# One decode block on one core: ten unread products more, other left-out rows in a gather, and wq loaded in two pieces

## The chip, the core and the metric

The kernel runs on one core of a Trainium2 chip. The metric is the device time of one execution in microseconds (us). Before the change it is 1305.99 us, the median of 3 runs (1305.94 to 1306.01).

## What is computed

One decode step of a transformer block in fp32 with a batch of 2, one new token each, model width 512, 32 heads of 128 and a cache of 8192 positions. The core of the reference:

```python
def _A_ref(x, k_cache, v_cache, wq, wo):
    q = (x @ wq).reshape(B, Sq, H, Dh).transpose(0, 2, 1, 3)
    scores = jnp.einsum("bhqd,bhkd->bhqk", q, k_cache) * (Dh ** -0.5)
    p = _softmax(scores, axis=-1)
    o = jnp.einsum("bhqk,bhkd->bhqd", p, v_cache)
    return o.transpose(0, 2, 1, 3).reshape(B, Sq, H * Dh) @ wo

def _B_ref(x, w1, b1, w2, b2):
    y = _layernorm(x, axis=-1)
    h = _gelu(jnp.einsum("bsd,df->bsf", y, w1) + b1)
    return jnp.einsum("bsf,fd->bsd", h, w2) + b2

h = x + _A_ref(_layernorm(x), k_cache, v_cache, wq, wo)
out = h + _B_ref(_layernorm(h), w1, b1, w2, b2)
```

k_cache and v_cache hold 2 x 32 x 8192 x 128 numbers each, 268 MB; wq (512 x 4096) and wo (4096 x 512) hold 8.39 MB each, w1 and w2 3.67 MB each. Each is read once, some 560 MB in all.

## The kernel before

**Units.** The heads are worked through in 32 units. A unit of the first 30 is a pair of heads for one batch entry (`units`, a pair g and a batch entry b), and the last two units are one head each for both entries. A unit's keys are one load of 8.39 MB, 128 partitions of 64 KB, and its values are another.

**Loads and slots.** All large loads go into a ring of three buffers of 64 KB per partition (`slot()`, name kv): wq first (lines 213 and 214), then each unit's k and v in turn, wo, and at the end the MLP's weights. `load` (L335) issues from SP, the last units' k and v from L347. A load into a buffer waits until the buffer's former content has been used. SP issues in program order; x alone is issued by ACT (L212), and the gather of wo by GpSimd. k of unit 0 comes in two halves, and the last loads (v of the last unit, L590, and w1 and w2, L601 to L606) in several pieces.

**The start.** x is normalized by VectorE and ScalarE and transposed by TensorE (L281). GpSimd makes the identity matrix, clears a few buffers and builds three placing matrices `pm` (L240 and L242: one copy for each run of kept rows) and `ioff` (L247). TensorE makes the gather's indices from them (L286), then all of q with 32 products (L308, 64 instructions) that each contract over the 128 partitions of wq; ScalarE copies it (L311), and `make_q` (L315) spreads one unit's q over the partitions (L325).

**One unit.** VectorE multiplies the keys by q in four chunks (`multiply`, L377), GpSimd adds the halves of three of the four (`halve`, L381), VectorE sums the rest (`add_up`, L384). After the second unit of a pair come the maximum over both (L394 to L404), the exponentials on ScalarE (`exps`, L421), and the products with the values on TensorE (`values`, L454). Unit i's last act is `spare(i)`, for i from 1 to 29: unread products of 2 x 2 into a corner of a buffer that is overwritten later (L332). `SPARE` of them are spread over the 29 units.

**wo and its gather.** The rows of wo for the last 8 of 28 heads are fetched by three indirect DMAs (`load_wo`, L358) in pieces of 4 rows, 8 KB per partition. `LEFT` lists, for each of the three, the partitions that are left out. Their index lies beyond the bounds check, so nothing is moved for them. `kept` turns each list into runs, and 256 of the 384 partitions are kept. The matrices `pm` put the attention output's rows on the partitions that are loaded. The three lists hold 128 partitions in all.

**The end.** The output of attention is projected (`project_all`, L524; the last two heads by L531 and the products at L675 and L678), the MLP follows (L689 to L710), and the result is written by SP (L714).

**Waits.** The class `Waits` (L40) sees each instruction as it is made and gives it the semaphores that it must wait for. DMAs from SP and ACT take eight semaphores (`by_hard_0` to `by_hard_7`) in turn, so a DMA also waits for the one issued eight before it, unless that is known to be done.

Of the kernel before, what the change touches and what calls it, by code (L numbers as in the profile page):

```python
# [12 lines left out]
P = 128  # L13
# [4 lines left out]
NG = 4  # L18
LH = 2
WARM = 3  # L20
SPARE = 412
GP = 5
SR = 4
LW = 4
LEFT = (((7, 10), (12, 16), (20, 28), (55, 56), (68, 92), (103, 104), (108, 109), (120, 121)),
        ((7, 9), (12, 17), (20, 28), (55, 56), (68, 92), (104, 105), (112, 113), (120, 121)),
        ((6, 9), (12, 16), (20, 28), (56, 57), (68, 92), (104, 105), (119, 120)))


def kept(left):  # L30
    at, runs, n = 0, [], 0
    for a, b in (*left, (P, P)):
        if a > at:
            runs.append((at, n, a - at))
            n += a - at
        at = b
    return runs, n
# [144 lines left out]
def tile_decode_block(nc, x, k, v, wq, wo, w1, b1, w2, b2, out):  # L182
# [3 lines left out]
    DC = D // P  # L186
# [21 lines left out]
    def slot():  # L208
        return kv.tile([P, ROW], F32, name="kv", tag="kv")
# [1 line left out]
    x2 = const.tile([B, D], F32, name="x2")  # L211
    nc.scalar.dma_start(x2, x.rearrange("b s d -> (b s) d"))  # L212
    wqt = slot()
    nc.sync.dma_start(wqt, wq.rearrange("(p r) n -> p (r n)", r=DC))
    wqs = wqt.rearrange("p (r n) -> p r n", r=DC)

    wol = wts.tile([P, LW, D], F32, name="wol")
# [8 lines left out]
    oall = const.tile([P, 2, 2 * GP, B], F32, name="oall")  # L226
    NQ = len(LEFT)
    og = const.tile([P, NQ * SR + LW - LH, B], F32, name="og")
    slots = [kept(x) for x in LEFT]
    first_slot = [2 * 2 * GP * P // SR + sum(n for _, n in slots[:q]) for q in range(len(LEFT))]  # L230
    HG = H - LW
# [4 lines left out]
    pms = {}  # L236
    for x in LEFT:
        if x not in pms:
            pms[x] = const.tile([P, P], F32, name=f"pm{len(pms)}")
            nc.gpsimd.memset(pms[x], 0.0)  # L240
            for p0, s0, n in kept(x)[0]:
                nc.gpsimd.tensor_copy(pms[x][:, p0:p0 + n], ident[:, s0:s0 + n])  # L242
    pm = [pms[x] for x in LEFT]
    FAR = 4096.0
    ioff = const.tile([P, len(LEFT)], F32, name="ioff")
    for q in range(len(LEFT)):
# [83 lines left out]
    def spare(i):  # L330
        for _ in range(SPARE * i // (NU - 3) - SPARE * (i - 1) // (NU - 3)):
            nc.tensor.matmul(rowacc[:, :B], wz, wz, start=True, stop=True)  # L332
# [408 lines left out]
```

## Time and profile before

| | |
|---|---|
| median of 3 runs | 1305.99 us |
| the profiled execution | 1305.84 us |
| its span, first to last instruction | 1304.4 us |
| TensorE clock granted, mean | 0.639 |
| busy: DVE / POOL / PE / ACT | 945.3 / 444.8 / 393.2 / 52.3 us |
| bytes read from HBM | 562.06 MB |

The profile covers one execution. Its times are microseconds from the span's start unless marked ns. PE is TensorE (PEld its weight loads), DVE VectorE, ACT ScalarE, POOL GpSimd, and SP the engine that issues most DMAs. A `q` behind a name (SPq) marks its queue of instructions that aren't counted as busy. L214 is line 214 of the kernel before. The bar of the span has 40 equal slices of 32.6 us. "DMA" in it is the mean busy share of the core's 16 DMA engines in tenths, and GB/s is what they moved. In a table by stage the share and the GB/s count a packet where it starts, so a short stage can show more than 1. The chain of waits is followed back from the last instruction to what released each step. "x64" is a count, and `sm<-ident,wol` reads: written tile, then the tiles read.

### The profile page before, as it was taken

What the parts mean: (1) busy time and instruction counts of PE and PEld (TensorE: products, weight loads), DVE (VectorE), ACT (ScalarE), POOL (GpSimd) and SP (SyncE); (2) the same over time, 40 slices, a digit from 0 to 9 for tenths busy, and PEclk for the clock granted to TensorE, in tenths of its full rate; (3) what the DMA queues carried; (4) which work ended last, traced back from release to release, by engine and by line L of the source; (5) the groups of instructions that cost most, each with busy time, mean ns of one, the idle gap of its engine ahead of it and who ended that gap; (6) DMA issues with size and microseconds to landing.
All of it is one profiled execution on the core that took longest, in us unless ns stands there. A gap on an engine that the chain in (4) does not pass through costs nothing.

```text
span 1304.4 us, 7121 instructions
## 1 busy us (share of the span) xinstructions
PE 393.2 (30%) x3134; PEld 127.1 (10%) x3135; DVE 945.3 (72%) x398; ACT 52.3 (4%) x173; POOL 444.8 (34%) x145
## 2 busy tenths in 40 slices
PE   3005033330412324033330503333041331403467
PEld 1001001010100101011110100101010110101113
DVE  1988777779777778777778877777976777877831
ACT  0010000000000000000000000000000000000011
POOL 2444432244432234432234442224442224444400
PEclk9557566665666657566665656657566665756687
DMA  9999999999999999999999999999999999999998
GB/s 402 434 450 419 444 424 441 429 437 432 436 431 433 436 431 435 432 428 437 431 436 430 435 434 434 435 429 441 420 447 418 449 420 441 425 430 432 421 435 366
DMA packets 12690, 561.46 MB, mean 430 GB/s; under 512 B 1504, under 2 KB 1520, under 8 KB 2676
## 3 DMA queue, kind: packets, MB, share of 16 engines
q1 hardware_dynamic: 12224, 558.92, 99.3%
q0 software_dynamic: 432, 2.10, 0.4%
q8 instruction: 24, 0.39, 0.1%
q14 instruction: 6, 0.05, 0.0%
q10 hardware_dynamic: 4, 0.00, 0.0%
HBM read 562.06 MB, written 0.00 MB: 431 GB/s over the span
## 4 chain that ended last, share of the span: by engine, by line
DMA 47%; DVE 38%; PE 13%; ACT 1%; POOL 1%; issue 0%; SPq 0%
DMA kv<-in_A_k_cache_dram 39%; DVE kv L377 22%; DVE s L384 14%; PE so L454 10%; DMA kv<-in_A_v_cache_dram 5%; DMA kv<-in_A_wq_dram 2%; DMA kv<-in_B_w_dram 1%; ACT pt L421 1%; PE so L308 1%; POOL kv L381 1%; PE sm L404 1%; DVE gm L401 0%; PE sm L396 0%; DVE orow L474 0%; DVE mx L394 0%
## 5 line engine op out<-in xcount | busy, mean ns | idle before, releaser
L377 DVE TENSOR_TENSOR kv<-kv,qps 128x4096 f32<-128x4096 f32 x128 | 564.0, 4408 | 286.3 <-DMA kv<-in_A_k_cache_dram 261.0
L381 POOL TENSOR_TENSOR kv<-kv 128x2048 f32<-128x2048 f32 x96 | 433.5, 4523 | 788.0 <-DVE kv L377 480.7
L454 PE MATMUL so<-kv,pt 128*16 128x512 f32 (+1 forms) x2048 | 289.1, 727 | 273.5 <-DMA kv<-in_A_v_cache_dram 251.4
L384 DVE TENSOR_REDUCE s<-kv 128x32 f32<-128x2048 f32 (+1 forms) x128 | 357.2, 2811 | 0.8 <-POOL kv L381 0.6
L396 PE MATMUL sm<-ident,mx 128*1 128x128 f32 x34 | 10.5, 318 | 539.3 <-DVE mx L394 539.3
L454 PEld LDWEIGHTS so<-kv,pt 128*16 128x16 f32 (+1 forms) x2048 | 63.7, 111 | 472.4 <-DMA kv<-in_A_v_cache_dram 255.0
L396 PEld LDWEIGHTS sm<-ident,mx 128*1 128x1 f32 x34 | 2.5, 79 | 546.8 <-DVE mx L394 542.7
L459 ACT ACTIVATE ss<-so 128x512 f32<-128x512 f32 x18 | 10.7, 597 | 575.2 <-PE so L454 540.7
L408 ACT ACTIVATE nb<-sm 128x4 f32<-128x4 f32 x15 | 2.6, 173 | 624.9 <-PE sm L404 624.9
L421 ACT ACTIVATE pt<-s,nb 64x128 f32<-64x128 f32 x60 | 23.9, 399 | 1.6
L401 DVE TENSOR_REDUCE gm<-sm 1x4 f32<-1x256 f32 (+1 forms) x17 | 7.0, 412 | 18.1 <-PE sm L396 18.1
L467 PE MATMUL sm<-ss,sel 128*4 128x128 f32 x120 | 15.6, 273 | 12.1 <-ACT ss L459 12.1
L332 PE MATMUL rowacc<-wz 128*2 128x2 bf16 x412 | 14.3, 163 | 0.0
L308 PE MATMUL so<-kv,yT 128*4 128x512 f32 x64 | 9.7, 776 | 14.1 <-DMA kv<-in_A_wq_dram 14.1
L325 PE MATMUL qps<-q,pick 4*128 4x128 f32 x60 | 12.1, 327 | 0.9 <-ACT q L311 0.9
L467 PEld LDWEIGHTS sm<-ss,sel 128*4 128x4 f32 x120 | 9.3, 87 | 27.8 <-ACT ss L459 25.9
L404 PE MATMUL sm<-gm,srow 1*128 1x4 f32 (+1 forms) x34 | 9.5, 348 | 8.1 <-DVE gm L401 8.1
L332 PEld LDWEIGHTS rowacc<-wz 128*2 128x2 bf16 x412 | 11.6, 81 | 1.7
L524 PE MATMUL so<-kv,oall 128*2 128x512 f32 x40 | 6.8, 844 | 15.0 <-DMA kv<-in_A_wo_dram 15.0
L421 ACT ACTIVATION_READ_ACCUMULATOR pt<-s,nb 64x1 f32 x60 | 11.1, 185 | 0.0
L486 PE MATMUL sm<-ident,orow 4*128 4x4 f32 x20 | 2.7, 257 | 25.2 <-DVE orow L474 25.2
L404 PEld LDWEIGHTS sm<-gm,srow 1*128 1x128 f32 x34 | 8.0, 292 | 13.6 <-DVE gm L401 13.6
(122 smaller groups left out, 123.8 us busy)
## 6 DMA issues: line engine op xcount, KB each, us to landing
kv<-in_A_k_cache_dram SPq DMA_DIRECT2D x6, 4096.0 KB, 34.4
kv<-in_A_v_cache_dram SPq DMA_DIRECT2D x3, 4096.0 KB
kv<-in_B_w_dram SPq DMA_DIRECT2D x3, 1792.0 KB, 13.9
kv<-in_A_wo_dram SPq DMA_DIRECT2D x1, 5120.0 KB
kv<-in_A_v_cache_dram SPq DMA_DIRECT2D x1, 2048.0 KB, 34.9
kv<-in_A_v_cache_dram SPq DMA_DIRECT2D x1, 1536.0 KB, 34.3
wol<-in_A_wo_dram SPq DMA_DIRECT2D x2, 512.0 KB, 41.0
kv<-in_B_w_dram SPq DMA_DIRECT2D x1, 768.0 KB, 14.8
```

Source lines behind the costliest of these rows:

```text
L308: nc.tensor.matmul(so2[0][32 * n:32 * n + 2 * B].rearrange("m (j d) -> m j d", d=DH), yT[:, r, (1 - e) * B:(3 - e) * B], wqe[:, r, n, e], ...
L325: nc.tensor.matmul(QP[g][:, b], w, q2[rows, j * DH:(j + 1) * DH], start=True, stop=True)
L332: nc.tensor.matmul(rowacc[:, :B], wz, wz, start=True, stop=True)
L377: nc.vector.tensor_tensor(kc, kc, QP[g][:, b, None, :].to_broadcast([P, CH, DH]), op=ALU.mult)
L381: nc.gpsimd.tensor_tensor(kc[:, :, 0:HP], kc[:, :, 0:HP], kc[:, :, HP:DH], op=ALU.add)
L384: nc.vector.tensor_reduce(S[i][:, c * CH:(c + 1) * CH], chunk(t, c)[:, :, 0:n], axis=AX.X, op=ALU.add)
L396: nc.tensor.transpose(MT[g][:, e, :], MX[g][:, e:e + 1], ident)
L404: nc.tensor.matmul(GM[g], srow, gm, start=True, stop=True)
L421: nc.scalar.activation(ptz[b][q, :, 4 * m:4 * m + 4], s[q], AF.Exp, bias=nb[q, b, e:e + 1], scale=SCALE, accum_out=lt4[q, m:m + 1])
L454: nc.tensor.matmul(so[32 * n:32 * n + w], p[:, u, cols], t[:, (at + u) * 512:(at + u + 1) * 512], start=(b == 0 and u < NG), stop=(b == B ...
L459: nc.scalar.activation(SS[g], so2[g % 2], AF.Copy)
L467: nc.tensor.matmul(OP[g], sel4[:, :, j], sj, start=(j == 0), stop=(j == 3))
```

## The change

Three constants or lines change. The number of unread products goes from 412 to 422. The lists of left-out partitions are others, with 43, 43 and 42 entries as before; the three lists now make 10, 9 and 10 runs of kept rows instead of 9, 9 and 8. wq is loaded by two DMAs in place of one: partitions 0 to 15, then 16 to 127. All lines from 215 on move down by one.

```diff
-SPARE = 412
+SPARE = 422
...
-LEFT = (((7, 10), (12, 16), (20, 28), (55, 56), (68, 92), (103, 104), (108, 109), (120, 121)),
-        ((7, 9), (12, 17), (20, 28), (55, 56), (68, 92), (104, 105), (112, 113), (120, 121)),
-        ((6, 9), (12, 16), (20, 28), (56, 57), (68, 92), (104, 105), (119, 120)))
+LEFT = (((7, 9), (12, 15), (16, 17), (20, 28), (56, 57), (68, 92), (103, 104), (108, 109), (119, 121)),
+        ((7, 9), (12, 15), (20, 28), (55, 57), (68, 92), (104, 105), (112, 113), (119, 121)),
+        ((8, 9), (12, 16), (20, 28), (55, 56), (68, 92), (103, 104), (108, 109), (112, 113), (120, 121)))
...
     wqt = slot()
-    nc.sync.dma_start(wqt, wq.rearrange("(p r) n -> p (r n)", r=DC))
+    for p0, p1 in ((0, 16), (16, P)):
+        nc.sync.dma_start(wqt[p0:p1], wq.rearrange("(p r) n -> p (r n)", r=DC)[p0:p1])
```

## Prediction

> **What bounds the kernel now.** I read first the page's bar of the span and its DMA queues, then the chain of waits, then busy time and DMA share by stage. Of the page:
>
> ```profile
> span 1304.4 us, 7121 instructions
> ...
> DMA  9999999999999999999999999999999999999998
> GB/s 402 434 450 419 444 424 441 429 437 432 436 431 433 436 431 435 432 428 437 431 436 430 435 434 434 435 429 441 420 447 418 449 420 441 425 430 432 421 435 366
> ...
> q1 hardware_dynamic: 12224, 558.92, 99.3%
> q0 software_dynamic: 432, 2.10, 0.4%
> q8 instruction: 24, 0.39, 0.1%
> ...
> HBM read 562.06 MB, written 0.00 MB: 431 GB/s over the span
> ```
>
> The 16 DMA engines have work all the time (99.3% plus 0.4% of 16 engines' span). By stage (columns: the stretch, its length, the five engines' busy time, the granted clock, the DMA share, GB/s):
>
> ```profile
> 10.00:22.00 12.00, 0.00 (x0) 0.00 (x0) 0.00 (x0) 0.00 (x0) 0.00 (x0) 1.00 0.93 401
> 22.00:33.00 11.00, 9.74 (x64) 1.77 (x64) 0.00 (x0) 0.43 (x1) 0.00 (x0) 1.00 1.00 432
> 33.00:1200.00 1167.00, 319.70 (x2558) 101.66 (x2558) 889.16 (x335) 41.87 (x151) 415.46 (x92) 0.62 1.00 433
> 1200.00:1285.00 85.00, 47.56 (x316) 14.14 (x316) 49.33 (x35) 5.17 (x15) 22.75 (x11) 0.71 0.99 421
> 1285.00:1301.00 16.00, 13.13 (x176) 7.26 (x171) 2.29 (x9) 3.31 (x5) 0.00 (x0) 0.79 0.98 407
> ```
>
> For 1167 us the share is 1.00 at 433 GB/s, while DVE, the busiest engine, works 889.16 of them (76%). So no engine bounds the kernel; the transfers do, and each waits only for the one ahead of it on its DMA engine. The two ends of the chain of waits (start, length, what):
>
> ```profile
> 0.74 21.90 DMA kv<-in_A_wq_dram
> 22.68 9.87 PE so L308 x64
> ...
> 105.18 34.83 DMA kv<-in_A_k_cache_dram
> ...
> 1285.76 15.99 DMA kv<-in_B_w_dram
> 1301.75 0.04 issue
> 1301.79 0.55 PE qps L710 x8
> ```
>
> The span begins with wq and ends 2.65 us after the last piece of w2 has landed (1304.4 less 1301.75). A k load issued at 105.18 lands 34.83 us later. Its own bytes, 8.39 MB at 433 GB/s, take 19.4 us; the other 15.4 us are transfers queued ahead of it. So a computation that is some us late costs nothing, but a microsecond in which all DMA engines move too little is never won back: it is added to the end.
>
> **The change part by part.** The sum is made against the profiled execution, 1305.84 us (span 1304.4 and 1.44 outside it); the median of the runs shown, 1305.99, is 0.15 above it.
>
> *wq in two pieces.* The reader's side first:
>
> ```profile
> L214 SPq DMA_DIRECT2D kv<-in_A_wq_dram x1: 398/398/398, 0.7 to 0.7; - x1
> ```
>
> ```profile
> 6.84 0.80 POOL L247 TENSOR_SCALAR ioff<-pidx 128x1 f32<-128x1 f32 x3
> ...
> 7.13 1.44 PE L286 MATMUL sm<-ioff,pm 128*128 128x1 f32 x6 [2.12 <-POOL ioff L247]
> ...
> 22.68 9.74 PE L308 MATMUL so<-kv,yT 128*4 128x512 f32 x64 [14.11 <-DMA kv<-in_A_wq_dram]
> ```
>
> No product begins sooner: each L308 product contracts over all 128 partitions, so the first waits for both pieces. Behind it on PE stands everything else; ACT's copy (L311) and DVE's first multiply wait for it. SP issues one DMA more (0.398 us by the row above), so k's first halves are issued 0.4 us later; wq keeps the DMA engines busy 20 us longer than that, so it costs nothing. The eight completion semaphores are taken in turn, and every later DMA moves on by one; the DMA whose completion each one waits for (eight back) stays the same.
>
> What matters is how fast 16 partitions are filled. 1.05 MB (16 x 64 KB) at 433 GB/s is 2.42 us, the other 112 are 17.0 us, together the 19.4 us of the whole. The trace has no such transfer: whatever carries weight covers 128 partitions, and the narrower ones are too small for a rate:
>
> ```profile
> kv<-in_B_b_dram SPq DMA_DIRECT2D x2, 7.0 KB
> kv<-in_B_b_dram SPq DMA_DIRECT2D x2, 2.0 KB
> x<-in_A_x_dram ACTq DMA_DIRECT2D x1, 4.0 KB
> ```
>
> So bounds. *Low end:* the engines set the rate, 16 rows go one to an engine, 2.42 us, loss 0. It can go below 0 by little: until 22 us the stages count 8.75 MB started (0.79 + 0.59 + 2.56 + 4.81 in the rows below and the one above), 20.2 us' worth, so 1.8 us are missing, 0.74 of them ahead of the issue; a sooner start is worth 1.1 us at most.
>
> ```profile
> 1.00:2.00 1.00, 0.00 (x0) 0.00 (x0) 0.84 (x5) 0.69 (x1) 0.99 (x3) 1.00 2.43 791
> 2.00:5.00 3.00, 0.60 (x4) 0.55 (x4) 1.82 (x7) 0.89 (x2) 2.87 (x21) 1.00 0.50 197
> 5.00:10.00 5.00, 1.44 (x7) 1.35 (x6) 1.36 (x8) 0.00 (x0) 2.34 (x15) 1.00 1.18 511
> ```
>
> *High end:* the 433 GB/s are 128 partitions' share together. Then 16 take 54 GB/s, 19.4 us, loss 17.0 us; and 112 take 379 GB/s, 19.4 us, loss 2.4 us. Together +19.4 us. All 16 engines are held: k0 and k1 are queued behind the pieces on the same engines. For the first piece I take the middle of its ends, 8.5 us: the nearest row in form (the whole wq) speaks for 0, but it covers eight times the partitions, and no row of such narrowness speaks. For the second piece I take 2.4 us: if partitions count at all, the 16 that it lacks do. Sum **+10.9 us**.
>
> [...]
>
> *Left-out rows.* Still 43, 43 and 42 of 3 x 128, so 256 rows of 8 KB are gathered as before; ten of the left-out rows are others. A row's price: 0.4% of 16 x 1304.4 us is 83 us, over 256 rows 0.33 us of one engine. Which engine carries which row the trace doesn't show: all ten on one engine would move the end by 3.3 us either way, evenly spread by nothing. The ten that come back lie between partitions 6 and 119, and so do the ten that go (16 to 120), so I take 0 and keep ±0.7 us (two rows on the engine that ends last). Three copies more build the placing matrices:
>
> ```profile
> L242 POOL COPY pm<-ident x26: 179/190/287, 2.6 to 6.6; 128x7 f32<-128x7 f32 x6, 128x12 f32<-128x12 f32 x4, 128x4 f32<-128x4 f32 x3, 128x11 f32<-128x11 f32 x3
> ```
>
> 3 x 0.19 = 0.57 us on POOL ahead of L247 and L286. PE idles 14.11 us after L286 until wq is there, so 0; with that cover gone, it would be 0.57.
>
> *Ten unread products.*
>
> ```profile
> L332 PEld LDWEIGHTS rowacc<-wz x412: 79/81/82, 104.9 to 1190.6; 128*2 128x2 bf16 x138
> L332 PE MATMUL rowacc<-wz x412: 163/163/164, 104.9 to 1190.6; 128*2 128x2 bf16 x138
> ```
>
> Ten times 0.163 + 0.081 is 2.4 us over 29 units, at most one product more in a unit. After them PE waits for v:
>
> ```profile
> PE so L454 <- DMA kv<-in_A_v_cache_dram: 251.4, 16, 17.4
> ```
>
> 251.4 us in 16 waits, 15.7 us each: hidden. Without that cover a load would be issued 0.24 us later, with 15.4 us queued ahead: still 0. Twenty more instructions may ask for one more of the 16 KB instruction packets (q8, 24 of 0.39 MB): 0.6 us on one engine, kept in the range.
>
> Sum: 1305.84 + 10.9 + 0 + 0 = 1316.74 in the profiled execution, 1316.9 as a median. Once the start is late, nothing after it is: v's first load is issued when wq's slot is free, 32.57 us before and some 43.5 now, with k0 and k1 (38.8 us of transfers) still in the queue until about 72.
>
> **The rivals.**
> 1. *No loss, not slower.* The engines alone set the rate, and 16 + 112 rows take 2.42 + 17.0 us in whatever pieces: 1306.0, with 1.1 us less at best for a sooner start and 0.7 + 0.6 us more for rows and a packet, 1304.9 to 1307.3. It decides if the first piece moves above about 200 GB/s (a loss under 2.6 us, 0.2% of the time, about what a measurement of this kernel can tell from no change). For it speaks that each engine still has eight rows of 64 KB, against it that then nothing would need 128 partitions. [...]
> 2. *Faster by over 0.2%.* The sooner start (1.1 us) and a better spread of rows at the end: the shares of 0.99 and 0.98 in the last two stages leave 0.85 + 0.32 = 1.2 us. Together 2.3 us, 1303.7, still within 0.2%: it decides only if both come whole and something more.
> [...]
>
> **How the numbers follow.** The forecast, a loss of 2.6 to 19.4 us: 0.60, its own range 1308.6 to 1325.4. No loss: 0.30, which is why the range begins at 1304.9. Over 0.2% faster: 0.04. More than 19.4 us: 0.06. The two last are left out. Slower 0.66, same 0.30, faster 0.04. [...]
>
> **What the profile after would show.** wq's second piece landing near 33.5 us instead of 22.64, L308 and the first DVE multiply as much later, the first GB/s slice far below 402 (about 260: 10.9 us of its 32.6 at 433 GB/s are 145 less), and after it the same 433 GB/s with a share near 1.00, and the last landing 11 us later. If wq lands at 22.6 again and the first slice holds 400, rival 1 is right and the forecast wrong by its largest term. [...] An L454 or SP wait that grows by microseconds would speak against my nothing for the products; a last stage whose share falls below 0.98 against my nothing for the rows.

## The result, and the profile after

The changed kernel takes 1328.03 us (median of 5 runs, 1327.20 to 1330.47), the kernel before, run beside it, 1306.01: the ratio is 1.0169, with a 95% interval of 1.0158 to 1.0180. It is slower by 22 us. The forecast was slower by 10.9 us, and the time lies 2.6 us above the end of its range.

The page of the changed kernel (lines from 215 on are one further down):

```profile
span 1325.9 us, 7146 instructions
...
DMA  9999999999999999999999999999999999999998
GB/s 214 366 429 442 435 421 437 441 422 432 443 430 431 433 437 432 430 437 430 433 433 435 433 433 430 433 437 432 426 439 439 424 431 443 430 423 434 422 431 358
...
q1 hardware_dynamic: 12240, 558.92, 99.2%
...
HBM read 562.06 MB, written 0.00 MB: 424 GB/s over the span
```

Two lines must be read against each other here. The DMA engines look busy throughout, as before: the bar shows 9 in every slice but the last. But GB/s is 214 in the first slice and 366 in the second, where it was 402 and 434. A packet takes longer here and counts as busy all the while: of the rows of wq (64 KB, one packet each) the first 16 took a median of 8.85 us, and the other 112, sixteen at a time in the order of their start, medians of 3.10 to 5.44, where the median of all 7680 packets of 64 KB is 2.42 in both kernels. So the busy share doesn't show this loss; the bytes do. Against the kernel before, (402 - 214 + 434 - 366) x 32.6 us is 8.3 MB, or 19 us at 433 GB/s (the slices of the two spans differ a little in length). By stage (stretch, length, busy times, granted clock, DMA share, GB/s):

```profile
2.00:12.00 10.00, 2.05 (x10) 1.91 (x10) 3.32 (x15) 0.88 (x2) 5.67 (x38) 1.00 0.89 144
12.00:22.00 10.00, 0.00 (x0) 0.00 (x0) 0.00 (x0) 0.00 (x0) 0.00 (x0) 1.00 0.80 211
22.00:32.00 10.00, 0.00 (x0) 0.00 (x0) 0.00 (x0) 0.00 (x0) 0.00 (x0) 1.00 0.94 236
32.00:42.00 10.00, 0.00 (x0) 0.00 (x0) 0.00 (x0) 0.00 (x0) 0.00 (x0) 1.00 0.94 223
42.00:52.00 10.00, 7.32 (x56) 1.57 (x60) 0.00 (x0) 0.00 (x0) 0.00 (x0) 1.00 0.96 406
...
200.00:500.00 300.00, 82.42 (x668) 26.29 (x660) 232.84 (x88) 8.80 (x31) 108.36 (x24) 0.62 1.00 433
500.00:800.00 300.00, 89.31 (x700) 27.30 (x699) 222.88 (x85) 10.93 (x40) 106.33 (x24) 0.63 1.00 433
800.00:1100.00 300.00, 87.67 (x711) 28.10 (x711) 222.48 (x86) 10.93 (x40) 99.40 (x23) 0.63 1.00 434
```

For 40 us the transfers go at about half of 433 GB/s or less, and in the long stages at 433 again. The two loads of wq, by their line (SP's time for each, and the time from issue to landing):

```profile
L215 SPq DMA_DIRECT2D kv<-in_A_wq_dram x2: 405/406/406, 0.7 to 1.2; - x2
...
DMA to landing us min/median/max: 12.4/27.9/43.4
```

The first piece, issued at 0.74, lands at 13.1, the second, issued at 1.2, at 44.6. Before, the whole of wq had landed at 22.64. The chain of waits, beginning and end:

```profile
0.74 12.36 DMA kv<-in_A_wq_dram
13.09 31.59 issue
44.69 8.57 PE so L309 x64
...
126.93 33.95 DMA kv<-in_A_k_cache_dram
...
1307.26 15.93 DMA kv<-in_B_w_dram
1323.19 0.04 issue
1323.24 0.55 PE qps L711 x8
```

The 31.59 us called "issue" are no issue. The first product waits for both pieces, by a wait of its own ahead of the product, and the chain follows the other one. L309's rows name it, 36.47 us from 8.2 to 44.7, the landing of the second piece:

```profile
L309 PEldq EVENT_SEMAPHORE  x1: 36473/36473/36473, 8.2 to 8.2; - x1
```

L309 begins 22.0 us later than L308 did (44.69 after 22.68), w2's last piece lands 21.4 us later (1323.19 after 1301.75), and the tail is 2.7 us as before. So the whole loss is there at 45 us, and 21.4 of the 22.0 us are still there when the last transfer lands.

### The profile page after: what moved, and what is told of

Read it like the earlier page. It is cut to its first block, busy times and chain, and to the rows that moved or that the text cites. A ratio compares the mean times of both kernels' runs of the same rounds, so it can differ in the third digit from the quotient of the medians.

```text
span 1325.9 us, 7146 instructions
## 1 busy us (share of the span) xinstructions
PE 398.0 (30%) x3145; PEld 128.3 (10%) x3145; DVE 945.3 (71%) x398; ACT 52.3 (4%) x173; POOL 445.1 (34%) x148
## 4 chain that ended last, share of the span: by engine, by line
DMA 45%; DVE 37%; PE 13%; issue 3%; ACT 1%; POOL 1%; SPq 0%
DMA kv<-in_A_k_cache_dram 38%; DVE kv L378 22%; DVE s L385 14%; PE so L455 10%; DMA kv<-in_A_v_cache_dram 5%; DMA kv<-in_B_w_dram 1%; ACT pt L422 1%; DMA kv<-in_A_wq_dram 1%; POOL kv L382 1%; PE so L309 1%; PE sm L405 1%; DVE gm L402 0%; PE sm L397 0%; DVE orow L475 0%; DVE mx L395 0%
## 5 line engine op out<-in xcount | busy, mean ns | idle before, releaser
L455 PE MATMUL so<-kv,pt 128*16 128x512 f32 (+1 forms) x2048 | 295.6, 740 | 270.7 <-DMA kv<-in_A_v_cache_dram 248.5
L309 PE MATMUL so<-kv,yT 128*4 128x512 f32 x64 | 8.4, 688 | 35.7 <-issue 35.7
```

Of the source, the lines that this page charges most:

```text
L309: nc.tensor.matmul(so2[0][32 * n:32 * n + 2 * B].rearrange("m (j d) -> m j d", d=DH), yT[:, r, (1 - e) * B:(3 - e) * B], wqe[:, r, n, e], ...
L455: nc.tensor.matmul(so[32 * n:32 * n + w], p[:, u, cols], t[:, (at + u) * 512:(at + u + 1) * 512], start=(b == 0 and u < NG), stop=(b == B ...
```

## Experiments

Each is compared with the kernel before, run on the same chip beside it.

**Which part of the change it is.** `split_alone` is the kernel before with the new two loads of wq and nothing else; `wq_whole` is the changed kernel with these undone:

```diff
-    for p0, p1 in ((0, 16), (16, P)):
-        nc.sync.dma_start(wqt[p0:p1], wq.rearrange("(p r) n -> p (r n)", r=DC)[p0:p1])
+    nc.sync.dma_start(wqt, wq.rearrange("(p r) n -> p (r n)", r=DC))
```

> The kernel before with wq in 16 and 112 partitions, and nothing else of the change. Theory (a load that covers fewer than 128 partitions is filled slowly, whatever else changes): the whole loss, 1328 us, within 1.5. Rival (the other left-out rows or the ten products carry part of it): clearly below 1327.

> The changed kernel with wq in one load of 128 partitions, so 422 products and the new left-out rows alone. Theory: 1306.0 within 0.7, the two other edits are worth nothing that counts. Rival: several us above or below 1306.

Measured: `split_alone` 1328.12 us, ratio 1.0168 (1.0153 to 1.0184); `wq_whole` 1306.12 us, ratio 1.0001 (0.9992 to 1.0010). The two loads of wq are the whole loss. The ten products and the other left-out rows are worth nothing to within 0.1%.

**Two loads, or their width.** `cut_columns` also loads wq by two DMAs with 1/8 and 7/8 of the bytes, but both cover all 128 partitions:

```diff
-    for p0, p1 in ((0, 16), (16, P)):
-        nc.sync.dma_start(wqt[p0:p1], wq.rearrange("(p r) n -> p (r n)", r=DC)[p0:p1])
+    for c0, c1 in ((0, ROW // 8), (ROW // 8, ROW)):
+        nc.sync.dma_start(wqt[:, c0:c1], wq.rearrange("(p r) n -> p (r n)", r=DC)[:, c0:c1])
```

> The changed kernel with wq still in two loads of 1/8 and 7/8 of its bytes, but cut across the columns: 8 KB and then 56 KB of each of the 128 partitions. Theory (the width counts): no loss, 1306 within 1. Rival (a second load at the head of the queue, or one DMA more on the eight semaphores, costs): near 1328.

Measured: 1306.56 us, ratio 1.0004 (0.9995 to 1.0013). Its chain of waits:

```profile
1.20 21.45 DMA kv<-in_A_wq_dram
22.69 9.70 PE so L309 x60
```

The second load, issued at 1.20, lands at 22.65, as the whole did. A DMA more at the head of the queue costs nothing, to within 0.13%; which partitions a load covers is what counts.

`halves` cuts the partitions in the middle instead (HP is 64):

```diff
-    for p0, p1 in ((0, 16), (16, P)):
+    for p0, p1 in ((0, HP), (HP, P)):
```

> The changed kernel with wq in partitions 0 to 63 and 64 to 127. [...] Rival (only the very narrow first piece and the 7 rows per engine of the second are slow): below +10 us, under 1316.

Measured: 1327.17 us, ratio 1.0165 (1.0150 to 1.0181), 21.1 us more. Two of its stages:

```profile
12.00:22.00 10.00, 0.00 (x0) 0.00 (x0) 0.00 (x0) 0.00 (x0) 0.00 (x0) 1.00 1.03 211
22.00:32.00 10.00, 0.00 (x0) 0.00 (x0) 0.00 (x0) 0.00 (x0) 0.00 (x0) 1.00 1.01 210
```

Half of the partitions at half the rate: 211 GB/s in place of 433. So slowness isn't a matter of a very narrow piece. It isn't one of fewer DMA engines either: eight engines at full speed would also move half, but then the mean share of the 16 would be near 0.5, and it is 1.03 and 1.01. A row of 64 KB, one packet, takes an estimated 5.1 us here (1.03 x 16 x 64 KB at 211 GB/s) where its median in the kernel before is 2.42. Two explanations are left. By *the share of partitions*, a load's rate is in proportion to the number of partitions it fills: each half takes 19.4 us instead of 9.7, 19.4 us more in all, near the 21.1 measured. By *place*, it goes by which partitions these are, so that another 64 could be filled faster.

**Each piece by itself.** These four are the kernel before with one more load ahead of wq, into the buffer that unit 1's keys overwrite later. The computation is untouched; what the load adds to the time is its own duration.

```diff
+    third = kv.held["kv"][1]
+    nc.sync.dma_start(third[0:16], wq.rearrange("(p r) n -> p (r n)", r=DC)[0:16])
     nc.sync.dma_start(wqt, wq.rearrange("(p r) n -> p (r n)", r=DC))
```

In `extra16_by8` the target is `third[0:P:8]`, in `extra112` it is `third[16:P]` with wq's rows 16 to 127, in `extra128` all of both.

> The kernel before, with wq whole, and ahead of it one more load of 16 rows of 64 KB (1.05 MB) into partitions 0 to 15 of a buffer that is overwritten later: the first piece by itself, its time added to 1306.1. Share of the partitions: 19.4 us, 1325.5. [...] Engines alone: 2.4 us, 1308.5.

> The same 1.05 MB into 16 partitions again, but every eighth one: 0, 8, 16 to 120. If only the number of partitions counts, as long as the 16 neighbours of the run beside it. [...] Engines alone: 2.4 us, 1308.5.

> The same with the second piece by itself: 112 rows (7.34 MB) into partitions 16 to 127. Share of the partitions: 19.4 us, 1325.5. If the piece is slow of itself, as in the changed kernel, where it landed 31.6 us after the first: 1337. If it was slow there only because the first had set the engines out of step: 17 to 19 us, 1323 to 1325.

> Control: the same with all 128 rows (8.39 MB) ahead of wq. Every theory: 19.4 us at 433 GB/s, 1325.5 within 1; if it is several us more, what the other three add isn't their transfer alone.

| | time, us | ratio (95%) | added, us | at 433 GB/s, us | lost, us |
|---|---|---|---|---|---|
| extra16 | 1315.36 | 1.0069 (1.0053 to 1.0086) | 9.1 | 2.4 | 6.7 |
| extra16_by8 | 1311.96 | 1.0045 (1.0028 to 1.0061) | 5.7 | 2.4 | 3.3 |
| extra112 | 1336.95 | 1.0234 (1.0217 to 1.0251) | 30.7 | 17.0 | 13.7 |
| extra128 | 1325.50 | 1.0147 (1.0130 to 1.0164) | 19.3 | 19.4 | 0 |

The control adds what its bytes take. Sixteen neighbours take 9.1 us and every eighth partition 5.7: the same bytes into the same number of partitions, in different times, both far from the 19.4 of the partitions' share and over the 2.4 of the engines alone. And the second piece is slow of itself, not because the first had set the engines out of step. The two losses make 20.4 of the 22 us.

**Place or share.** The next three keep the number of partitions and move them: `extra64_low` to `third[0:64]`, `extra64_mid` to `third[32:96]`, `extra16_by4_mid` to `third[32:96:4]`, with wq's first 64 or 16 rows.

> The kernel before with one more load ahead of wq: 64 rows of 64 KB (4.19 MB) into partitions 0 to 63 of a buffer that is overwritten later. Share of the partitions: 64 of 128, half rate, 19.4 us, 1325.6. [...] Engines alone: 9.7 us, 1315.9.

> The same 64 rows into partitions 32 to 95. Share of the partitions: again 19.4 us, 1325.6. [...]

> 16 rows (1.05 MB) into every fourth partition from 32 to 92. Share of the partitions: 19.4 us, 1325.6. If wider spacing helps by itself: between the 9.1 us of partitions 0 to 15 and the 5.7 us of every eighth, so over 5 us. [...]

Measured: `extra64_low` 1326.42 us, ratio 1.0155 (1.0138 to 1.0172), 20.4 us added; `extra64_mid` 1317.05, ratio 1.0083 (1.0066 to 1.0100), 11.0 added; `extra16_by4_mid` 1308.63, ratio 1.0019 (1.0009 to 1.0028), 2.6 added. The rows of the load's line, in this order:

```profile
DMA to landing us min/median/max: 23.1/23.1/23.1
```

```profile
DMA to landing us min/median/max: 12.4/12.4/12.4
```

```profile
DMA to landing us min/median/max: 5.2/5.2/5.2
```

and those of `extra16` and `extra16_by8`:

```profile
DMA to landing us min/median/max: 12.2/12.2/12.2
```

```profile
DMA to landing us min/median/max: 7.8/7.8/7.8
```

The same 4.19 MB into as many neighbouring partitions land in 23.1 us at 0 to 63 and in 12.4 at 32 to 95. The same 1.05 MB land in 12.2, 7.8 or 5.2 us by place alone. The share of the partitions is refuted: by it each of these loads takes 19.4 us, and 64 partitions added 11.0 us where 433 GB/s would take 9.7, and 16 added 2.6 where it would take 2.4. So the place counts. What makes one place slower than another the runs don't show.

`mid_first` begins with the 64 partitions that were filled fast:

```diff
-    for p0, p1 in ((0, 16), (16, P)):
+    for p0, p1 in ((32, 96), (0, 32), (96, P)):
```

> The changed kernel with wq in three pieces: partitions 32 to 95, then 0 to 31, then 96 to 127. [...] Share of the partitions: three times 19.4 us, +38.8, 1345.

Measured: 1317.61 us, ratio 1.0087 (1.0070 to 1.0104), 11.5 us more than before, 9.6 less than the two halves. Its stages:

```profile
2.00:12.00 10.00, 2.05 (x10) 1.90 (x10) 3.29 (x15) 0.88 (x2) 5.57 (x38) 1.00 1.04 420
12.00:22.00 10.00, 0.00 (x0) 0.00 (x0) 0.00 (x0) 0.00 (x0) 0.00 (x0) 1.00 0.99 210
22.00:32.00 10.00, 0.00 (x0) 0.00 (x0) 0.00 (x0) 0.00 (x0) 0.00 (x0) 1.00 1.02 213
```

64 partitions at 420 GB/s, then 32 and 32 at half of it: more pieces and narrower ones, and less loss.

**112 and 96 partitions, 13 further down.** Two more loads move the slow second piece, 112 rows to `third[3:115]` and 96 to `third[3:99]`:

> The kernel before with one more load of 112 rows (7.34 MB) ahead of wq, into partitions 3 to 114 instead of 16 to 127. [...]

> The same with 96 rows (6.29 MB, 14.5 us at full rate), six an engine, into partitions 3 to 98. [...]

Measured: 1335.86 us, ratio 1.0221 (1.0204 to 1.0239), 29.8 us added; and 1336.27, ratio 1.0227 (1.0210 to 1.0244), 30.2 added. The 112 rows are about as slow as at 16 to 127 (30.7), and 96 take as long as 112. Three stages of `extra96_at3`:

```profile
12.00:17.00 5.00, 0.00 (x0) 0.00 (x0) 0.00 (x0) 0.00 (x0) 0.00 (x0) 1.00 1.00 210
17.00:22.00 5.00, 0.00 (x0) 0.00 (x0) 0.00 (x0) 0.00 (x0) 0.00 (x0) 1.00 1.01 210
22.00:27.00 5.00, 0.00 (x0) 0.00 (x0) 0.00 (x0) 0.00 (x0) 0.00 (x0) 1.00 0.97 210
```

The sum over all engines stays at 210 GB/s, about half of 433. The trace's records of the single packets show more. Taken sixteen at a time in the order of their start, the rows of 64 KB in these loads took, as a median and in us:

| | median time of a row, step by step, us |
|---|---|
| extra112 | 4.66, 4.78, 3.47, 3.14, 4.52, 4.74, 4.49 |
| extra112_at3 | 3.27, 3.28, 4.70, 4.73, 3.23, 4.42, 4.74 |
| extra96_at3 | 4.72, 4.81, 5.11, 4.94, 5.10, 4.79 |

Five steps take 3.1 to 3.5 us and the other 15 take 4.4 to 5.1, where a row's median in the kernel before is 2.42. The rows of a step are slow together: in those 15 steps the fastest row of all took 4.0 us. This also accounts for 96 rows taking as long as 112: each of their six steps is a slow one, while two or three of the seven steps of 112 rows are shorter. The medians add up to 29.8, 28.4 and 29.5 us, near the 30.7, 29.8 and 30.2 that the loads added. Which engine carries which row isn't in the trace; what holds the rows up, and why some steps are shorter, stays open.

## Why the prediction was right and wrong

*The bound* was right. The transfers set the end: 22.0 us lost before L309 are 21.5 us of the span, with 433 GB/s in the long stages of both kernels.

*Products and left-out rows*: 0 forecast, with ±0.7 us and a packet's 0.6 kept. Measured together 0.05 us, within ±0.1%.

*Sooner start, issue, semaphores*: nothing forecast, nothing found to within 0.13% (`cut_columns`).

*The first piece*: 8.5 us of loss taken, 6.7 measured by itself. The middle of two bounds came near, by luck as much as by reason: the runs refute both, the engines alone (0) and the partitions' share (17.0). In `extra16` 1.05 MB in 9.1 us are 115 GB/s.

*The second piece* is where it failed: "For the second piece I take 2.4 us: if partitions count at all, the 16 that it lacks do." It lost 13.7 us by itself, and about 14.5 in the changed kernel (31.5 us between the two landings, less 17.0). The step priced how many partitions are reached, and the runs show that this number isn't the price: in a whole load of 128 a row takes 2.42 us, in one of 112 (`extra112`) 3.1 to 4.8, though the load covers seven eighths, and 64 partitions from 32 to 95 added 11.0 us, 1.3 more than their bytes take at 433 GB/s. A loss of more than 19.4 us was given 0.06, and the prediction states no reason for so little.

*The range* failed by the same step. Its end, +19.4 us, was the partitions' share for both pieces, taken as the worst case; `extra112` alone lost 13.7 where that bound allowed 2.4.

*Rival 1*, that the engines alone set the rate, is out: the same bytes in 12.2 and 5.2 us. *Rival 2* had nothing to stand on, as the start wasn't sooner: the first piece landed at 13.1 us, and no product could begin before the second.

*What the profile was to show*: wq landing near 33.5 us (44.6), the first GB/s slice near 260 (214, and 366 in the second), 433 after it with a share near 1.00 (so in the long stages), the last landing 11 us later (21.4). PE's wait for v at L454 didn't grow (248.5 us after 251.4). The share of the last stage did fall, to 0.95 from 1306 to 1322 us, the sign against nothing for the rows. It speaks of something else: the share falls as well in `split_alone`, where the rows are the old ones (0.95 in the same stretch), and stays at 0.98 in `wq_whole` (1285 to 1301 us), where rows and products are the new ones.

## What to carry to other kernels

Where transfers bound a kernel, cut a load across the columns rather than across the partitions: here the cut by columns cost nothing and the cuts by partitions 11.5 to 22 us. If a load must be narrow, place it: here 64 partitions from 32 to 95 landed in 12.4 us and 0 to 63 in 23.1. Don't take the number of partitions for a price: 112 of 128 added 30.7 us for 17.0 us' worth of bytes. Look for such a loss in GB/s and in the time from issue to landing; the DMA engines' busy share didn't show it (1.03 and 1.01 at 211 and 210 GB/s in `halves`).

## What was not expected of the hardware

- Sixteen partitions were filled in 9.1, 5.7 or 2.6 us by which ones they were (0 to 15, every eighth, every fourth from 32 to 92).
- 112 and 96 partitions went at about half rate (30.7 or 29.8 us, and 30.2, for 17.0 and 14.5 us' worth of bytes).
- Sixteen rows in a step were slow together: in 15 steps of 20 the median row took 4.4 to 5.1 us and the fastest of all 4.0, in the other five the median was 3.1 to 3.5, and it is 2.42 in the kernel before.
